# A gated attention and mixer kernel: w2's last 128 columns turned for three chunks, two weight loads later, the last output in three transfers

## The chip, the cores and the metric

The kernel runs on one core of one Trainium2 chip. The time is the device time of one execution in microseconds (us), and what is compared is the median of several runs.

## The reference, cut to what matters

The input x has 2048 tokens of 640 numbers (bfloat16). Two branches read it and a gate mixes them:

```python
g = sigmoid((x * gate_w).sum(-1))
a = linear_attention(x, wqkv) @ wo               # 32 heads of 20, phi(t) = t + 1 or exp(t)
h = gelu(layernorm(x) @ w1)
hs = shifted(h) @ w2                             # quarters of h's columns moved by +1, -1, +2, -2 tokens
x1 = x + hs
b = x1 + gelu(layernorm(x1) @ w3) @ w4           # w3 is 640 x 1728, w4 is 1728 x 640
out = g * a + (1 - g) * b
```

The change edits `x1 = x + hs`, the sums that the second layernorm takes from x1, and the moments at which w3 and w4 are loaded and the output's last tile is stored.

## The kernel before, in words

**Tiles.** Tokens are worked in 16 tiles of 128 and 4 chunks of 512; columns of 640 are 5 blocks of 128. Up to the second layernorm a chunk c has these steps, named as the planner's items are:

- `t1(u)`: a crossbar transpose (a DMA on SP's queue) of a normalized tile into `xnT`, so that columns lie on partitions.
- `w1(c, j)`, j = 0 to 4: five matmuls of 512 columns on TensorE (PE); ScalarE (ACT) takes the result through GELU into `hsT`, with the shift of tokens in the address. For j = 4 that is four pieces of 32 partitions.
- `w2(t)`: tile t's product with w2. For each of five blocks of `hsT` a matmul of 512 columns (L624), and one of the last 128 columns (L613) that keeps the same weights. VectorE (DVE) adds the 640 columns to `x_tok` and sums them for the layernorm (L662).
- `sq(t)`: ACT squares the tile and sums the squares (L680).
- `s2(c)`: GpSimd (POOL) makes mean and scale of four tiles from the sums, in eight small steps (`ln_chunk_stats`).
- `n2(u)`: POOL normalizes tile u into one of three buffers `xn`; `n2(u)` needs the buffer of `t2(u-3)` free.
- `t2(u)`: the crossbar transpose of that tile into `xnT`.
- `w3(c, j)`, j = 0 to 12: five matmuls of 512 columns (L605), GELU on ACT into `h2T`.

A chunk's last w2 tile needs the next chunk's last w1 group as well, for the shifted tokens. `w3(0, 3)` needs `w2(15)`.

**The attention branch meets this one** in the tiles `a(t)` (L1240), five matmuls each of `pqnT` with the small matrix `M_sb`. `pqnT` lies in the same memory as `hsT`. It is made by `qs(t)` and `qn(t)` on DVE (some 2.9 us a tile) and by the crossbar transpose `qt(t)`, which needs `w2(15)` and, for t < 6, `t2(11)`. Rows 60 to 67 of `M_sb` are copied from `Mt` by `mt`, five small DMAs on SP, planned after `qt(2)`. `qt(3)` and `t2(12)` are planned after `mt`. `w3(1, 7)` to `w3(1, 10)` are planned after `a(0)` to `a(3)`, one each; w4's products come after that.

**Order of work.** The program for each engine is written out by a planner at build time. It holds streams of items (W1, W2, SQ, S2, N2, T2, W3 and so on). Within a stream the order is fixed. Each item has a PE duration (1.08 for five matmuls of 512 columns, 1.33 for a w2 tile, 0 for an item without PE work) and dependencies with a lag (GEL = 1.3 behind a w1 group). The planner keeps a model of the engines' clocks. It issues the item that can start first by that model; among those, items without PE work go first, then the item with the longest remaining path of durations and lags:

```python
key = (max(est, t_pe), 0 if it["dur"] == 0.0 else 1, -cp[n])
```

On the chip every engine and every DMA queue then runs its list in order and waits on semaphores. So an instruction that waits holds up all that was planned behind it on its engine. SP's queue carries the crossbar transposes, the large loads of w3 and w4 and the output; the planner's model lets a crossbar land 2.8 us after its issue, whatever else is in flight.

**A turned product** exists already in the kernel for w4's last 128 columns (`w4_turned`): w4's block is the weights and 512 tokens are streamed. The result, with columns on partitions, goes through ACT into `mw` and by a crossbar transpose into `mtok`, four tiles at once, and DVE adds each tile's 128 columns.

**Loads.** w3 (one DMA, 2160 KB) and w4 (three DMAs, 2080 KB and twice 80 KB) are issued on SP, both before at about 89 us, behind `qb(3)` and `t1(15)`.

**The end.** The last tile's w4 product lies in two parts of PSUM, columns 0 to 384 and 384 to 512; the 128 turned columns are added first. Its output goes out in two transfers, columns 0 to 384 from ACT's queue and 384 to 640 from SP's.

Of the kernel before, what the change touches and what calls it, by code (L numbers as in the profile page):

```python
# [7 lines left out]
ACTF = mybir.ActivationFunctionType  # L8
ALU = mybir.AluOpType

S = 2048
D = 640
# [3 lines left out]
NT = S // 128  # L16
NCH = S // 512
KD = D // 128
# [398 lines left out]
def _build(nc, A_x, A_wqkv, A_wo, B_w1, B_w2, B_w3, B_w4, gate_w, out, dbg=None, stop=None):  # L417
    sch = _Sched(nc)
# [41 lines left out]
    ps = nc.alloc_psum_tensor("ps", [128, 8, 512], F32)  # L460
# [10 lines left out]
    st2 = pa.alloc("st2", [128, 8, NT], F32)  # L471
# [4 lines left out]
    w2 = pa.alloc("w2", [128, KD, D], BF16)  # L476
    wo_aug = pa.alloc("wo_aug", [128, 6, D], BF16)
    x_tok = pa.alloc("x_tok", [128, NT, D], BF16)
    xnT = pa.alloc("xnT", [128, KD, S], BF16)
    hsT = pa.alloc("hsT", [128, KD, S + 4], BF16)  # L480
# [28 lines left out]
    mw = rb.alloc("mw", [128, 2, 512], BF16)  # L509
    mtok = rb.alloc("mtok", [128, 2, 4, 128], BF16)  # L510
# [8 lines left out]
    def bank():  # L519
        best = None  # L520
        for k_ in range(nbanks[0]):
            b = (bank_rr[0] + k_) % nbanks[0]
            if b in bank_pend or b in bank_hold:
                continue
            lk = sch.locks.get(b)
            tfree = 0.0 if lk is None else sch.ev_time.get((lk[1].sem, lk[1].val), 1e18)
            if best is None or tfree < best[0]:
                best = (tfree, b)
        bank_rr[0] = best[1] + 1
        bank_pend.add(best[1])  # L530
        return best[1]
# [30 lines left out]
    def nfree(ap):  # L562
        n = 1
        for d_ in ap.shape[1:]:
            n *= d_
        return n

    def in_psum(ap):
        return ap.tensor.name == ps.name
# [8 lines left out]
    def dve(fn, reads, writes, cost=None):  # L578
        if cost is None:
            n = nfree(writes[0])  # L580
            cost = 65.0 + n / 0.96
        return sch.op("dve", fn, reads, writes, cost=cost)
# [7 lines left out]
    def pe(fn, reads, writes, cost=500.0, after=None):  # L590
        for w_ in writes:
            sp_, rl = sch.rects(w_)
            if sp_ == "ps":
                for (_p0, _p1, lo, hi) in rl:
                    for b in range(lo // PS_BANK, (hi - 1) // PS_BANK + 1):
                        bank_pend.discard(b)
        return sch.op("pe", fn, reads, writes, cost=cost, after=after)

    def mm_group(out_ap, pairs, reads_extra=()):
        n = len(pairs)  # L600

        def fn(e, out_ap=out_ap, pairs=pairs, n=n):
            ins = None
            for i, (l, r) in enumerate(pairs):
                ins = e.matmul(out_ap, l, r, start=(i == 0), stop=(i == n - 1))  # L605
            return ins
        reads = [a for p in pairs for a in p] + list(reads_extra)
        return pe(fn, reads, [out_ap], cost=n * (max(nfree(pairs[0][1]), 24) * 0.4167 + 2.5))
# [40 lines left out]
    def tt(engf, out_ap, a, b_, op):  # L649
        cost = None  # L650
        if engf is pool:
            cost = 1000.0 if op == ALU.pow else 200.0 + 2.3 * nfree(out_ap)
        elif not in_psum(a):
            cost = 830.0
        return engf(lambda e: e.tensor_tensor(out_ap, a, b_, op), [a, b_], [out_ap], cost=cost)  # L655

    def stt(out_ap, in0, scalar, in1, op0, op1, accum=None):
        rd = [in0, in1] + ([scalar] if not isinstance(scalar, (int, float)) else [])
        n = nfree(out_ap)
        cost = (65.0 + n / 0.96) if (in_psum(in0) or in_psum(in1)) else (160.0 + 1.04 * n)  # L660
        if accum is not None:
            return dve(lambda e: e.scalar_tensor_tensor(out_ap, in0, scalar, in1, op0, op1, accum_out=accum), rd,  # L662
                       [out_ap, accum], cost=cost + 70.0)
        return dve(lambda e: e.scalar_tensor_tensor(out_ap, in0, scalar, in1, op0, op1), rd, [out_ap], cost=cost)  # L664
# [3 lines left out]
    def activation(out_ap, in_ap, func, scale=1.0, bias=0.0, accum=None):  # L668
        rd = [in_ap] + [a for a in (scale, bias) if not isinstance(a, (int, float))]
        wr = [out_ap] + ([accum] if accum is not None else [])  # L670
        n = nfree(out_ap)
        cost = max(150.0, 100.0 + 0.833 * n + (70.0 if in_psum(in_ap) else 0.0)) + 45.0 * (len(rd) - 1)
        if accum is not None:
            cost += 91.0
        st_ = ACT_SET.get(func)
        if st_ is not None and st_ != sch.act_func:
            cost += 1290.0
            sch.act_func = st_
        if accum is not None:
            return act(lambda e: e.activation(out_ap, in_ap, func, bias=bias, scale=scale, accum_out=accum), rd, wr, cost=cost)  # L680
        return act(lambda e: e.activation(out_ap, in_ap, func, bias=bias, scale=scale), rd, wr, cost=cost)  # L681
# [106 lines left out]
    def tag_set(buf, sl, what):  # L788
        tags[(buf, sl)] = what

    def tag_chk(buf, sl, what):
        assert tags.get((buf, sl)) == what, ("stale ring slot", buf, sl, what, tags.get((buf, sl)))

    IT = _Items()
# [65 lines left out]
    def ln_chunk_stats(st, c, rs):  # L860
        cs = slice(4 * c, 4 * c + 4)
        ts(pool, st[:, 2, cs], rs, 1.0 / D, 0.0, ALU.mult, ALU.add)
        ts(pool, st[:, 3, cs], st[:, 1, cs], 1.0 / D, EPS_LN, ALU.mult, ALU.add)
        tt(pool, st[:, 4, cs], st[:, 2, cs], st[:, 2, cs], ALU.mult)
        tt(pool, st[:, 5, cs], st[:, 3, cs], st[:, 4, cs], ALU.subtract)
        tt(pool, st[:, 6, cs], st[:, 5, cs], negh[:, 0:4], ALU.pow)
        tt(pool, st[:, 7, cs], st[:, 2, cs], st[:, 6, cs], ALU.mult)
        ts(pool, st[:, 7, cs], st[:, 7, cs], -1.0, 0.0, ALU.mult, ALU.add)
# [101 lines left out]
    for i in range(3, NT + 2):  # L970
        if i < NT:
            addA(("q", i), 1.08, lambda t=i: q_tile(t))
            addA(("k", i), 1.36, lambda t=i: k_tile(t))
            if i % 4 == 3:
                addA(("qx", i // 4), 1.08, lambda c=i // 4: q_turned(c))
                IT.add("QB", ("qb", i // 4), 0.0, lambda c=i // 4: q_back(c),
                       deps=[(("qx", i // 4), 2.5), (("t1", NT - 1), 0.0) if i == NT - 1 else (("k", i + 1), 0.0)])
# [140 lines left out]
    def w2_tile(t):  # L1118
        tok = slice(2 + 128 * t, 2 + 128 * (t + 1))
        b = pair()  # L1120
        mm_both((ps[:, b, 0:512], ps[:, b + 1, 0:128]), [(hsT[:, k, tok], w2[:, k, 0:512], w2[:, k, 512:D]) for k in range(KD)])
        stt(x_tok[:, t, :], psf[:, 512 * b:512 * b + D], 1.0, x_tok[:, t, :], ALU.mult, ALU.add, accum=st2[:, 0, t:t + 1])

    def w2_sq(t):
        activation(junk[:, 0, :], x_tok[:, t, :], ACTF.Square, accum=st2[:, 1, t:t + 1])

# [206 lines left out]

    def out_tiles(t0, t1):
        dst = out[0, 128 * t0:128 * t1, :].rearrange("(n p) d -> p n d", p=128)
        for n0, n1 in ((0, 384), (384, D)) if t0 == NT - 1 else ((0, D),):
            sch.dma("act" if n1 == 384 else "sp", dst[:, :, n0:n1], x_tok[:, t0:t1, n0:n1], "out%d" % slot("out", 4))

    def w3_load():
# [9 lines left out]
    for c in range(NCH):  # L1349
        for j in range(KD):  # L1350
            deps = [(("t1", u), 0.9) for u in range(4 * c, 4 * c + 4)] if j == 0 else []
# [7 lines left out]
    for t in range(NT):  # L1359
        c = t // 4  # L1360
        deps = [(("w1", c, KD - 1), GEL)]
        if t % 4 == 3 and c + 1 < NCH:
            deps.append((("w1", c + 1, KD - 1), GEL))
        if t == 0:
            deps.append((("g", KD - 1), 0.0))
        IT.add("W2", ("w2", t), 1.33, lambda t=t: w2_tile(t), deps)
        IT.add("SQ", ("sq", t), 0.0, lambda t=t: w2_sq(t), [(("w2", t), 1.0)])
        if t % 4 == 3:
            IT.add("S2", ("s2", c), 0.0, lambda c=c: ln_chunk_stats(st2, c, st2[:, 0, 4 * c:4 * c + 4]), [(("sq", t), 1.0)])
    for u in range(NT):  # L1370
        deps = [(("s2", u // 4), 3.2 + 0.9 * (u % 4))]
        if u >= 3:
# [2 lines left out]
            deps.append((("t1", NT - 3 + u), 0.0))  # L1375
        IT.add("N2", ("n2", u), 0.0, lambda u=u: normalize(2, u, st2), deps)
        IT.add("T2", ("t2", u), 0.0, lambda u=u: t_xn(2, u), deps=[(("n2", u), 1.1)] + ([(("mt",), 0.0)] if u == 12 else []))
    IT.add("MISC", ("w3load",), 0.0, w3_load, deps=[(("qb", NCH - 1), 0.0), (("k", NT - 1), 0.0), (("t1", NT - 1), 0.0)])
    IT.add("MISC", ("w4load",), 0.0, w4_load, deps=[(("qb", NCH - 1), 0.0), (("kvt", 1), 0.0), (("t1", NT - 1), 0.0), (("z", NT - 1), 1.5)])
    for c in range(NCH):  # L1380
        for j in range(KFF):
            deps = []
# [4 lines left out]
            if j == 0:  # L1387
                deps = deps0 + [(("t2", u), 0.9) for u in range(4 * c, 4 * c + 4)]
# [12 lines left out]
    for t in range(NT):  # L1401
        deps = [(("zb",), 1.0), (("q", max(t, 2)), 2.0), (("sg", 1), 0.0)]
# [13 lines left out]
    for t in range(NT):  # L1416
        g = GOF[t]
        t0, t1 = GROUPS[g]
        cl = (t1 - 1) // 4
        deps = [(("qt", t), 3.0), (("w4load",), 0.0), (("m", 1), 1.0), (("mt",), 2.5)]  # L1420
# [66 lines left out]
```

## Time and profile before

| | us |
|---|---|
| median of 3 runs | 259.79 (259.15 to 259.86) |
| the profiled execution | 259.33 |
| its span, first to last instruction | 258.1 |
| PE busy | 255.2 |
| DVE busy | 143.3 |
| ACT busy | 108.5 |
| POOL busy | 90.1 |

PE's granted clock is full in every slice of the page. "PE" is the matmul stream and "PEld" the weight loads, which run beside it. A matmul of 512 columns is listed with 379 ns, but the matmuls are pipelined: the step from one start to the next is what it costs the stream. In a timeline each row has start, length, engine, line, operation, operands and count; `[idle ... <-...]` tells how long the engine stood still before it and what ended that. "SPq" is SP's queue; an issue's row has the time that issuing took, and the landing comes later. The median from issue to landing is 2.7 us for `xnT<-xn`, 2.4 us for `mtok<-mw`, 8.2 us for w3's load and 13.8 us for w4's largest.

### The profile page before, as it was taken

The page shows a single profiled execution, that of the slowest core. Times are in us where ns is not written, and L with a number is a line of the kernel's source. Part 1 is how long each engine was busy: PE and PEld are TensorE (multiplying, and loading weights), DVE is VectorE, ACT ScalarE, POOL GpSimd, SP SyncE. Part 2 cuts the span into 40 slices and gives each one's busy share as a digit, 9 for nine tenths or more (in the row PEclk, how much of TensorE's full clock was granted, in tenths as well). Part 3 has the DMA queues.
Part 4 walks back from the last instruction along what each step waited for, and adds up shares of the span by engine and source line. Part 5 has one row for each costly group of instructions (what it writes and reads, how often), then busy time and mean ns, then how long its engine had stood idle before and what let it go on. Part 6 is the DMA issues. An engine that isn't in the chain of part 4 may idle for free.

```text
span 258.1 us, 3609 instructions
## 1 busy us (share of the span) xinstructions
PE 255.2 (99%) x1418; PEld 111.0 (43%) x1242; DVE 143.3 (56%) x289; ACT 108.5 (42%) x222; POOL 90.1 (35%) x146
## 2 busy tenths in 40 slices
PE   8999999999999999999999999999999999999996
PEld 4333333344444333334444444444444444444444
DVE  2697888899953995489999400689300043200033
ACT  1496676751356867665854230003520100253000
POOL 5021399966772153667917100423000011300000
PEclk9999999999999999999999999999999999999999
DMA  6855599956843699562556631022300112200012
GB/s 206 245 136 105 180 182 131 268 116 127 109 97 79 97 338 358 106 101 56 108 55 125 122 61 20 0 79 76 51 0 0 23 20 102 102 1 3 0 20 102
DMA packets 57681, 26.48 MB, mean 103 GB/s; under 512 B 48916, under 2 KB 56253, under 8 KB 57664
## 3 DMA queue, kind: packets, MB, share of 16 engines
q1 hardware_dynamic: 54832, 21.87, 38.5%
q0 software_dynamic: 1168, 3.28, 5.8%
q10 hardware_dynamic: 1664, 1.11, 1.5%
q8 instruction: 10, 0.16, 0.3%
q14 instruction: 7, 0.06, 0.1%
HBM read 12.04 MB, written 2.62 MB: 57 GB/s over the span
## 4 chain that ended last, share of the span: by engine, by line
PE 99%; DVE 0%; issue 0%
PE ps L605 37%; PE ps L1240 30%; PE ps L624 14%; PE ps L831 7%; PE ps L613 4%; PE ps L942 2%; PE ps L904 1%; PE ps L1286 1%; PE ps L1147 1%; PE ps L636 1%; PE ps L1029 0%; PE ps L1058 0%; DVE x_tok L664 0%
## 5 line engine op out<-in xcount | busy, mean ns | idle before, releaser
L605 PE MATMUL ps<-xnT,w 128*128 128x512 bf16 x360 | 81.3, 379 | 0.0
L664 DVE SCALAR_TENSOR_TENSOR x_tok<-ps,stg,abx 128x512 bf16<-128x512 f32 (+2 forms) x17 | 12.2, 718 | 81.7 <-PE ps L1240 81.5
L681 ACT ACTIVATE h2T<-ps 128x512 bf16<-128x512 f32 x52 | 30.6, 598 | 59.3 <-PE ps L605 59.3
L605 PEld LDWEIGHTS ps<-xnT,w 128*128 128x128 bf16 x360 | 34.5, 98 | 41.6 <-issue 2.4
L1240 PE MATMUL ps<-w,h2T 128*128 128x512 bf16 (+2 forms) x221 | 45.4, 366 | 0.0
L647 POOL TENSOR_SCALAR xn<-x_tok,st 128x640 bf16<-128x640 bf16 x32 | 34.9, 1096 | 28.2 <-DMA xnT<-xn 27.6
L647 POOL TENSOR_SCALAR abx<-x_tok,stg 128x640 f32<-128x640 bf16 (+1 forms) x16 | 14.8, 933 | 70.2 <-DVE x_tok L664 70.2
L1240 PEld LDWEIGHTS ps<-w,h2T 128*128 128x128 bf16 x221 | 21.1, 98 | 24.1
L681 ACT ACTIVATE Er<-ps 128x512 bf16<-128x512 f32 (+1 forms) x36 | 23.0, 648 | 15.0 <-PE ps L613 10.7
L680 ACT ACTIVATE junk<-x_tok 128x640 bf16<-128x640 bf16 x32 | 23.6, 738 | 3.9 <-DVE x_tok L662 3.7
L681 ACT ACTIVATE hsT<-ps 128x512 bf16<-128x512 f32 (+1 forms) x32 | 19.0, 594 | 12.5 <-PE ps L605 12.0
L624 PE MATMUL ps<-w,hsT 128*128 128x512 bf16 x80 | 23.0, 379 | 0.0
L624 PE MATMUL ps<-wkg,xT 128*128 128x512 bf16 x70 | 20.7, 379 | 0.0
L662 DVE SCALAR_TENSOR_TENSOR x_tok<-ps,x_tok 128x640 bf16<-128x640 f32 x16 | 13.2, 822 | 11.0 <-PE ps L613 10.5
L1240 PE MATMUL ps<-M_sb,pqnT 128*128 128x512 bf16 (+2 forms) x85 | 18.6, 367 | 0.0
L831 PE MATMUL ps<-pk_tok,x_tok 128*128 128x512 bf16 x80 | 17.8, 379 | 0.0
L1176 DVE TENSOR_TENSOR pq_tok<-pq_tok,dnr 128x300 bf16<-128x300 bf16 (+1 forms) x48 | 17.4, 417 | 0.6
L613 PE MATMUL ps<-wkg,xT 128*128 128x130 bf16 x80 | 17.5, 219 | 0.0
L613 PE MATMUL ps<-w,hsT 128*128 128x128 bf16 x80 | 17.5, 219 | 0.0
L605 PE MATMUL ps<-wq,xT 128*128 128x512 bf16 x65 | 16.1, 379 | 0.0
L647 DVE TENSOR_SCALAR Er<-Er 128x512 bf16<-128x512 bf16 (+1 forms) x36 | 12.2, 339 | 7.0 <-ACT Er L681 6.3
L655 DVE TENSOR_TENSOR qprod<-qprod,pk_tok 128x640 f32<-128x640 f32 x13 | 15.2, 1166 | 0.4
(90 smaller groups left out, 252.6 us busy)
## 6 DMA issues: line engine op xcount, KB each, us to landing
w<-in_B_w_dram SPq DMA_DIRECT2D x1, 2160.0 KB, 8.2
w<-in_B_w_dram SPq DMA_DIRECT2D x1, 2080.0 KB, 13.8
out_dram<-x_tok SPq DMA_DIRECT2D x3, 640.0 KB, 3.2
w<-in_B_w_dram POOLq DMA_DIRECT2D x8, 160.0 KB, 6.2
x_tok<-in_A_x_dram SPq DMA_DIRECT2D x6, 160.0 KB, 3.9
x_tok<-in_A_x_dram SPq DMA_DIRECT2D x1, 960.0 KB, 5.4
wv<-in_A_wqkv_dram POOLq DMA_DIRECT2D x1, 800.0 KB, 5.6
x_tok<-in_A_x_dram SPq DMA_DIRECT2D x1, 640.0 KB, 4.6
```

Of the source, the lines that this page charges most:

```text
L605: ins = e.matmul(out_ap, l, r, start=(i == 0), stop=(i == n - 1))
L613: return e.add_instruction(mybir.InstMatmult(name=nc.get_next_instruction_name(), engine=e.engine, ins=[e.lower_ap(r), ll], outs=[e.lower_ ...
L624: e.matmul(outs[0], l, r, start=st, stop=sp, skip_group_check=True)
L647: return engf(lambda e: e.tensor_scalar(out_ap, in_ap, s1, s2, op0, op1), rd, [out_ap], cost=cost)
L655: return engf(lambda e: e.tensor_tensor(out_ap, a, b_, op), [a, b_], [out_ap], cost=cost)
L662: return dve(lambda e: e.scalar_tensor_tensor(out_ap, in0, scalar, in1, op0, op1, accum_out=accum), rd, [out_ap, accum], cost=cost + 70.0)
L664: return dve(lambda e: e.scalar_tensor_tensor(out_ap, in0, scalar, in1, op0, op1), rd, [out_ap], cost=cost)
L680: return act(lambda e: e.activation(out_ap, in_ap, func, bias=bias, scale=scale, accum_out=accum), rd, wr, cost=cost)
L681: return act(lambda e: e.activation(out_ap, in_ap, func, bias=bias, scale=scale), rd, wr, cost=cost)
L831: ins = e.matmul(o, l, r, start=(t0 + q_ == 0), stop=(t0 + q_ == NT - 1))
L1176: dve(lambda e, o=o, i0=i0, i1=i1: e.tensor_tensor(o, i0, i1, ALU.mult), [i0, dnr[:, 1, sd, :]], [o], cost=cost)
L1240: ins = e.matmul(o, l, r, start=first and i == 0, stop=last and i == len(prs) - 1, skip_group_check=True)
```

## The change

For chunks 0 to 2, a w2 tile multiplies only the first 512 columns (`w2_wide`); after a chunk's fourth tile one turned group (`w2_turned`, item `w2x(c)`) makes the last 128 columns for the chunk's 512 tokens. ACT copies it to `mw`, SP transposes it into `mtok`, and DVE adds it tile by tile (`w2_tail`, item `wt(u)`) with a sum of its own. The squares `sq(u)` of these tiles follow `wt(u)`, and `s2(c)` first adds the two sums on POOL. Chunk 3 stays as it was. w3's load is planned after `w2x(0)`, w4's after `w2x(2)` and `t2(7)`. The last tile's output goes out in three transfers: the turned columns 512 to 640 on SP, 0 to 384 on ACT, 384 to 512 on SP.

```diff
@@ -1121,6 +1121,33 @@
         mm_both((ps[:, b, 0:512], ps[:, b + 1, 0:128]), [(hsT[:, k, tok], w2[:, k, 0:512], w2[:, k, 512:D]) for k in range(KD)])
         stt(x_tok[:, t, :], psf[:, 512 * b:512 * b + D], 1.0, x_tok[:, t, :], ALU.mult, ALU.add, accum=st2[:, 0, t:t + 1])
 
+    W2T = 3
+
+    def w2_wide(t):
+        tok = slice(2 + 128 * t, 2 + 128 * (t + 1))
+        b = bank()
+        mm_group(ps[:, b, :], [(hsT[:, k, tok], w2[:, k, 0:512]) for k in range(KD)])
+        stt(x_tok[:, t, 0:512], ps[:, b, :], 1.0, x_tok[:, t, 0:512], ALU.mult, ALU.add, accum=st2[:, 0, t:t + 1])
+
+    def w2_turned(c):
+        sl = c % 2
+        b = bank()
+        mm_group(ps[:, b, :], [(w2[:, k, 512:D], hsT[:, k, 2 + 512 * c:2 + 512 * (c + 1)]) for k in range(KD)])
+        activation(mw[:, sl, :], ps[:, b, :], ACTF.Copy)
+        tag_set("mtok", sl, ("w2", c))
+        sch.dma("sp", mtok[:, sl, :, :], mw[:, sl, :], "trw%d" % sl, transpose=True)
+
+    def w2_tail(t):
+        c = t // 4
+        tag_chk("mtok", c % 2, ("w2", c))
+        stt(x_tok[:, t, 512:D], mtok[:, c % 2, t % 4, :], 1.0, x_tok[:, t, 512:D], ALU.mult, ALU.add, accum=st2[:, 3, t:t + 1])
+
+    def w2_sums(c):
+        cs = slice(4 * c, 4 * c + 4)
+        if c < W2T:
+            tt(pool, st2[:, 0, cs], st2[:, 0, cs], st2[:, 3, cs], ALU.add)
+        ln_chunk_stats(st2, c, st2[:, 0, cs])
+
     def w2_sq(t):
         activation(junk[:, 0, :], x_tok[:, t, :], ACTF.Square, accum=st2[:, 1, t:t + 1])
 
@@ -1333,7 +1360,7 @@
 
     def out_tiles(t0, t1):
         dst = out[0, 128 * t0:128 * t1, :].rearrange("(n p) d -> p n d", p=128)
-        for n0, n1 in ((0, 384), (384, D)) if t0 == NT - 1 else ((0, D),):
+        for n0, n1 in ((512, D), (0, 384), (384, 512)) if t0 == NT - 1 else ((0, D),):
             sch.dma("act" if n1 == 384 else "sp", dst[:, :, n0:n1], x_tok[:, t0:t1, n0:n1], "out%d" % slot("out", 4))
 
     def w3_load():
@@ -1363,10 +1390,17 @@
             deps.append((("w1", c + 1, KD - 1), GEL))
         if t == 0:
             deps.append((("g", KD - 1), 0.0))
-        IT.add("W2", ("w2", t), 1.33, lambda t=t: w2_tile(t), deps)
-        IT.add("SQ", ("sq", t), 0.0, lambda t=t: w2_sq(t), [(("w2", t), 1.0)])
+        turned = c < W2T
+        IT.add("W2", ("w2", t), 1.08 if turned else 1.33, lambda t=t: (w2_wide if t // 4 < W2T else w2_tile)(t), deps)
+        if turned and t % 4 == 3:
+            IT.add("W2", ("w2x", c), 1.08, lambda c=c: w2_turned(c), deps)
+            for u in range(4 * c, 4 * c + 4):
+                IT.add("WX", ("wt", u), 0.0, lambda u=u: w2_tail(u), [(("w2x", c), 3.6)])
+                IT.add("SQ", ("sq", u), 0.0, lambda u=u: w2_sq(u), [(("wt", u), 0.4)])
+        if not turned:
+            IT.add("SQ", ("sq", t), 0.0, lambda t=t: w2_sq(t), [(("w2", t), 1.0)])
         if t % 4 == 3:
-            IT.add("S2", ("s2", c), 0.0, lambda c=c: ln_chunk_stats(st2, c, st2[:, 0, 4 * c:4 * c + 4]), [(("sq", t), 1.0)])
+            IT.add("S2", ("s2", c), 0.0, lambda c=c: w2_sums(c), [(("sq", t), 1.0)])
     for u in range(NT):
         deps = [(("s2", u // 4), 3.2 + 0.9 * (u % 4))]
         if u >= 3:
@@ -1375,8 +1409,8 @@
             deps.append((("t1", NT - 3 + u), 0.0))
         IT.add("N2", ("n2", u), 0.0, lambda u=u: normalize(2, u, st2), deps)
         IT.add("T2", ("t2", u), 0.0, lambda u=u: t_xn(2, u), deps=[(("n2", u), 1.1)] + ([(("mt",), 0.0)] if u == 12 else []))
-    IT.add("MISC", ("w3load",), 0.0, w3_load, deps=[(("qb", NCH - 1), 0.0), (("k", NT - 1), 0.0), (("t1", NT - 1), 0.0)])
-    IT.add("MISC", ("w4load",), 0.0, w4_load, deps=[(("qb", NCH - 1), 0.0), (("kvt", 1), 0.0), (("t1", NT - 1), 0.0), (("z", NT - 1), 1.5)])
+    IT.add("MISC", ("w3load",), 0.0, w3_load, deps=[(("qb", NCH - 1), 0.0), (("k", NT - 1), 0.0), (("t1", NT - 1), 0.0), (("w2x", 0), 0.0)])
+    IT.add("MISC", ("w4load",), 0.0, w4_load, deps=[(("qb", NCH - 1), 0.0), (("kvt", 1), 0.0), (("t1", NT - 1), 0.0), (("z", NT - 1), 1.5), (("w2x", 2), 0.0), (("t2", 7), 0.0)])
     for c in range(NCH):
         for j in range(KFF):
             deps = []
```

## The prediction

> **What bounds the kernel now.** I read the page first: its head and the chain that ended last.
>
> ```profile
> span 258.1 us, 3609 instructions
> ...
> PE 99%; DVE 0%; issue 0%
> ```
>
> TensorE carries the end: 99% of the chain. Only matmul columns taken away, or a gap in the matmul stream, can move the time. Next the busy time by stretch, over the stage that the change edits (81 to 118 us) and the one behind it:
>
> ```profile
> 81.00:109.40 28.40, 28.40 (x178) 10.93 (x122) 20.73 (x50) 19.16 (x40) 10.54 (x20) 1.00 0.78 216
> 118.30:138.70 20.40, 20.40 (x109) 9.15 (x108) 19.39 (x45) 14.27 (x29) 11.22 (x16) 1.00 0.52 85
> ```
>
> The columns are the stretch, its length, busy PE, PEld, DVE, ACT, POOL, the clock and the DMA share with GB/s. PE is busy without a hole at clock 1.00, so there is no stall to win back. DVE is nearly full in the second stretch (19.39 of 20.40). Then PE's timeline where the last w1 group (L605 x5) gives way to w2 tiles 10 and 11:
>
> ```profile
> 106.92 1.24 PE L605 MATMUL ps<-xnT,w 128*128 128x512 bf16 x5
> 108.00 0.38 PE L624 MATMUL ps<-w,hsT 128*128 128x512 bf16 x1
> 108.22 0.22 PE L613 MATMUL ps<-w,hsT 128*128 128x128 bf16 x1
> 108.27 0.38 PE L624 MATMUL ps<-w,hsT 128*128 128x512 bf16 x1
> ...
> 109.36 2.32 PE L605 MATMUL ps<-xnT,w 128*128 128x512 bf16 x10
> 111.52 0.38 PE L624 MATMUL ps<-w,hsT 128*128 128x512 bf16 x1
> ```
>
> A 512-column matmul costs 0.216 us from start to start (108.00 to 108.22), the 128-column one behind it 0.055, a tile 1.36 (108.00 to 109.36). The two groups at 109.36 are already w3(0,0) and w3(0,1): they fill the time in which tile 11 waits for ScalarE's view of the last w1 group:
>
> ```profile
> 108.20 2.44 ACT L681 ACTIVATE hsT<-ps 32x512 bf16<-32x512 f32 x4 [1.12 <-PE ps L605]
> ```
>
> Last I looked for what becomes due after the stage. PE's first attention tile a(0) reads M_sb, whose rows 60 to 67 come by five small DMAs on SP's queue; behind that queue stands GpSimd's normalization:
>
> ```profile
> 114.86 0.54 POOL L647 TENSOR_SCALAR st<-st 128x4 f32<-128x4 f32 x1 [0.66 <-ACT junk L680]
> ...
> 118.27 2.61 POOL L647 TENSOR_SCALAR xn<-x_tok,st 128x640 bf16<-128x640 bf16 x3
> 121.83 1.80 POOL L647 TENSOR_SCALAR xn<-x_tok,st 128x640 bf16<-128x640 bf16 x1 [0.94 <-DMA xnT<-xn]
> ```
> ```profile
> 119.18 5.67 SPq L281 DMA_TRANSPOSE xnT<-xn  x4
> 124.89 3.92 SPq L281 DMA_TRANSPOSE pqnT<-pq_tok  x3
> 128.91 4.07 SPq L285 DMA_DIRECT2D M_sb<-Mt  x5
> ```
> ```profile
> 138.51 1.24 PE L1240 MATMUL ps<-M_sb,pqnT 128*128 128x512 bf16 x5
> ```
>
> SP runs in order and back to back here: t2(8..11), qt(0..2), M_sb. t2(11) is the fourth transpose; it starts at 123.65 (the 1.20 us before 124.89, and a 0.04 gap). M_sb's last issue ends at 132.98; with 1.6 us of landing (the 64 KB output's row) M_sb is there at 134.6. PE asks at 138.5. **So the slack of t2(11) is 3.9 us**, and w3(1,7) is held behind a(0) in the items' dependencies: PE has nothing else then.
>
> **The change, part by part.** *PE's columns.* Per chunk, 20 matmuls of 128 columns (20 x 0.056 = 1.12 us) go and 5 of 512 come (5 x 0.216 = 1.08): the same columns. Gain 0.04 a chunk, 0.13 us in all. (The Trainium skill, "TensorE: Matmul & The Clock Gate", section "Back-to-back issue gap", gives about 81 ns for a 128-column matmul in a stream with its weight loads; by that the gain would be 60 x 0.081 - 3.24 = 1.6 us. The row says 0.055, as the second matmul here keeps the weights, so the rule is not used.)
>
> *Order on PE.* The planner issues by longest remaining path, with its own costs; I use these for order alone. The turned path adds 1.08 + 3.6 + 0.4 to a chunk, yet w1 and w2 still merge one by one. Through tile 10, eleven tiles lose 0.28 each and two turned groups add 1.08 each: tile 10 ends at 109.36 - 0.95 = 108.4. The last w1 group now ends two wide tiles earlier, 106.25, and its hsT is ready 2.65 later (108.00 to 110.64 before): 108.95. w3(0,0) can't fill the hole, since chunk 0's t2(3) comes later than 108.5 (next part). **A gap of 0 to 0.55 us; I take 0.55.** Tile 11 ends at 110.0, the turned group of chunk 2 at 111.1, tiles 12 to 15 at 116.6.
>
> *Chunk 0's and 1's longer path* (copy, crossbar, tail add, square) delays t2(0..3) from 108.5 to about 113 to 117 and t2(4..7) from 117 to about 123. PE has tiles 12 to 15 until 116.6 and w3's chunk 0 (13 x 1.08) until 131. The crossbar of chunk 2 stands ahead of t2(3) on SP and waits for ACT's copy; PE may wait up to 0.5 us there, which the next part swallows. Nothing else is charged.
>
> *Chunk 2's path, where the money is.* Before: tile 11 ended at 112.88, t2(11) started at 123.65. Now from 111.1:
> - Copy on ACT: 0.2 + 0.6 gives 111.9 at once; behind chunk 1's four squares, ready just before (four of 0.92, 0.73 + 0.19, from 108.95), 113.2. I take 113.2.
> - Crossbar 0.1 + 2.4 (row of mtok): 114.4 to 115.7.
> - Four tail adds on DVE, 0.34 + 0.08 each, 1.7: 116.1 if they go at once; behind the adds of tiles 12 to 15, the last ending at 116.6 + 0.2 + 0.8 = 117.6, 119.3. I take 119.3: when the planner's crossbar lands, tile 15 is already issued.
> - Squares: the last 0.92 behind its add, 117.0; or four in a row from 118.1 with two GELUs of w3 (0.5 each) between them, 122.7. I take 122.7.
> - GpSimd's sums: 114.86 to 118.27 was 3.4, and one 0.2 is added: 120.6 to 126.3.
> - n2(8) 0.9, t2(8) 2.6 to land, n2(11), which reuses that buffer, 0.9 (the row at 118.27, a third of 2.61) to 1.8 (the row at 121.83), 0.1: t2(11) at 125.1 to 131.7. I take 0.9 as the commoner, so 130.8.
> - The queue behind it as before, 123.65 to 134.6 = 10.9: M_sb at 136.0 to 142.6, by my choices **141.7**. PE asks at 138.5 - 0.1 + 0.55 = 138.9.
>
> So PE idles between nothing and 3.7 us at a(0), and I take 2.8: three of the four choices (squares ahead, adds ahead, ACT full) follow from in-order queues that were full in the profile.
>
> *The loads.* w3's (one DMA) is issued behind the first crossbar, about 94 instead of 89.5, and lands 8.2 later, 14 us before its first use. w4's (three DMAs) goes behind t2(7), about 122, needed at 151.7; even 13.8 us is enough. But they share SP's queue:
>
> ```profile
> w<-in_B_w_dram SPq DMA_DIRECT2D x1, 2080.0 KB, 13.8
> ```
> ```profile
> DMA to landing us min/median/max: 4.2/6.6/7.6
> ```
>
> The second line is the transposes issued at 97 to 103, in the shadow of the two loads; those at 119 to 124 took 2.6 (all four). The shadow moves from t2(0..2) to t2(8..10). Alone, w4's 2.1 MB at some 300 GB/s (2160 KB and 2080 KB landed by 104 after 89.5) takes 7 us, to 129: t2(8), issued at 127, lands 0 to 2 us later than counted. I take 0; 2 goes into the range.
>
> *Output.* The last transfer shrinks from 64 to 32 KB. By the rows (64 KB 1.6, 96 KB 1.7, 160 KB 1.8) that gives 0.05 us; one more issue on SP (0.4) lies earlier. Bounds -0.1 and +0.1. (The Trainium skill, "DMA: Bandwidth & Descriptors", "Specifications", puts the line rate at 512 bytes or more, with a read-modify-write below; the rows of 128 columns now are 256 bytes, so by it the sum would gain nothing here. No row of before has such an output.)
>
> **Sum**, on the profiled execution's own 259.33 us (span 258.1 and 1.2 around it): -0.13 + 0.55 + 2.8 - 0.05 = +3.2, 262.5. The median of the runs, 259.79, lies 0.46 above that execution; shifted by that the forecast is **263.0 us**.
>
> **Rivals.** *Not slower: the slack holds.* If the tail adds get ahead of tiles 12 to 15 on DVE and the squares run as they land, t2(11) starts by 127.9 (123.65 + 3.9 + the 0.4 that PE is later) and a(0) finds M_sb. For it: the low ends above give 125.1, and tile 11 itself runs 2.9 us earlier. Against: all three queues must be free at once. Then the time is 259.79 - 0.18 to + 0.37: 259.6 to 260.2. Chance 0.24. *The load in the way.* At 90.67 in SP's timeline an issue of w4 lasted 5.5 us behind w3's load. If SP stands like that behind w4's load, or t2(8) lands 5 late (7.6 against 2.6), t2(11) moves to 133 or more and a(0) to 144: 265 to 266. Against: w3's bytes are gone by then. Chance 0.13. *The change does nothing on PE*: a turned group has the columns of what it replaces, which is the 0.13 already in the sum; it can't be over 0.2, so faster by 0.3% (0.78 us, about what a measurement of this kernel can tell from no change) needs a gain that no row shows: 0.03. The forecast case, 1 to 4 us of waiting, has 0.60.
>
> Range: 259.6 to 265.0. It takes in the holding case, leaves out the gain and most of the load case, some 2 in 10. The forecast case's own range is 261 to 264.5. Same takes 0.23, slower 0.74.
>
> **What would show it.** Right: PE's first hole at about 108.4, up to 0.6 us, released by ACT hsT; a hole of 2 to 4 us before the first M_sb<-pqnT matmul, released by DMA M_sb; M_sb's five issues at 136 to 141 instead of 129 to 133; t2(8..11) at 127 to 131; 60 hsT matmuls fewer on L613, 15 more of 512 columns on L605. From there to the end the stream must keep its length (119.6 us from 138.5). Wrong: PE at 99 to 100% through 139 us, or the hole elsewhere, for instance at w3(0,0) near 116.6 for w3's load, or t2(11) before 128 although the squares ran late.

## The result and the profile after

The changed kernel takes 267.38 us (median of 6 runs, 265.97 to 268.46), the kernel before 259.7 us beside it: a ratio of 1.0301, 95% interval 1.0273 to 1.0329. The forecast was 263.0 us with a range up to 265.0: slower, as forecast, but by 7.7 us and not by 3.2. The profiled execution of the changed kernel is the slowest of the six, 268.46 us; its own excess over the profiled execution of before (259.33) is 9.1 us.

The page of the kernel after, its head, two of its 40-slice rows and the chain that ended last:

```profile
span 267.2 us, 3601 instructions
...
PE   8899999999999999999893999999999999999997
...
PEclk9999999999999999999997799999999999999999
...
PE 90%; ACT 5%; issue 2%; DMA 2%; SPq 0%; DVE 0%; ACTq 0%
```

A slice is 6.7 us. The PE row has a notch, 8 9 3, in the slices from 127 to 147 us; the clock row has 7 7 in the two from 140 to 154 us, where before it had nines throughout. PE carries 90% of the chain instead of 99%. The waits of PE, with total, number and longest in us:

```profile
PE ps L1267 <- issue: 4.6, 1, 4.6
PE ps L1058 <- ACT h2T L681: 1.0, 1, 1.0
...
PE ps L605 <- ACT hsT L681: 0.4, 1, 0.4
```

L1267 is the line that was L1240 before. PE's timeline shows where they lie:

```profile
106.46 2.32 PE L605 MATMUL ps<-w,hsT 128*128 128x512 bf16 x10
109.15 1.04 PE L605 MATMUL ps<-w,hsT 128*128 128x512 bf16 x4 [0.36 <-ACT hsT L681]
...
128.70 0.74 PE L1058 MATMUL ps<-wo_aug,Lt 60*64 60x512 bf16 x16 [0.99 <-ACT h2T L681]
129.37 10.96 PE L605 MATMUL ps<-xnT,w 128*128 128x512 bf16 x50
144.91 2.29 PE L1267 MATMUL ps<-M_sb,pqnT 128*128 128x512 bf16 x5 [4.58 <-issue]
147.00 2.34 PE L605 MATMUL ps<-xnT,w 128*128 128x512 bf16 x5
```

Three holes. Measured as steps from start to start beyond what the matmul costs, they are 0.53 us behind 108.40, 1.16 behind 127.33 and 4.74 behind 139.96. The last ends with a(0), the first M_sb<-pqnT matmul, at 144.91 instead of 138.51. And the five matmuls of a(0) take 2.29 us where before five took 1.24. The windows around a(0) say why (columns as in the prediction: stretch, length, busy PE, PEld, DVE, ACT and POOL, clock, DMA share and GB/s):

```profile
140.20:144.90 4.70, 0.13 (x1) 0.02 (x1) 4.46 (x11) 0.60 (x1) 0.74 (x1) 0.89 0.06 13
144.90:148.10 3.20, 3.19 (x8) 1.14 (x9) 3.06 (x8) 0.00 (x0) 0.00 (x0) 0.50 0.70 139
148.10:151.20 3.10, 3.10 (x9) 1.07 (x8) 0.76 (x3) 0.60 (x1) 0.87 (x2) 0.58 0.60 120
151.20:160.00 8.80, 8.80 (x49) 3.98 (x49) 0.00 (x0) 3.04 (x6) 0.77 (x1) 1.00 0.63 125
```

PE stood for 4.7 us, and then the granted clock is half for some six microseconds: 8 matmuls in 3.20 us, where at full clock 15 would go. The loss is (1 - 0.50) x 3.20 + (1 - 0.58) x 3.10 = 2.9 us, with PE listed as fully busy.

So the 9.1 us of the profiled execution are in two parts. a(0) is 6.4 us later: 0.2 because the work before the edited stage lies that much later in this execution (50.80 instead of 50.63 for the same matmul), +0.5, +1.2 and +4.7 for the holes, and -0.13 for the columns. From a(0) to the end it takes 122.3 us (267.2 - 144.91) instead of 119.6: +2.7, the clock.

SP's queue shows what a(0) waited for:

```profile
113.36 1.19 SPq L281 DMA_TRANSPOSE mtok<-mw  x1
116.48 5.43 SPq L281 DMA_TRANSPOSE xnT<-xn  x4
121.96 2.19 SPq L285 DMA_DIRECT2D w<-in_B_w_dram  x3
126.96 8.39 SPq L281 DMA_TRANSPOSE xnT<-xn  x4
135.39 3.92 SPq L281 DMA_TRANSPOSE pqnT<-pq_tok  x3
139.41 4.21 SPq L285 DMA_DIRECT2D M_sb<-Mt  x5
```

t2(8..11) took 8.39 us of the queue instead of 5.67, M_sb's five issues end at 143.62 instead of 132.98. The trace names no releaser for a(0) (`issue`). That it is M_sb shows in the order of times: here and in nine of the kernels below, all those with a hole at a(0), it starts 1.2 to 1.3 us after the end of M_sb's fifth issue, and in qt_early and msb_first the row names DMA M_sb. Two views more belong to this lateness. The landing of the three transposes issued from 127.0 to 129.5, t2(8..10):

```profile
DMA to landing us min/median/max: 3.9/4.7/5.2
```

and POOL's timeline over the same time:

```profile
125.64 3.02 POOL L647 TENSOR_SCALAR xn<-x_tok,st 128x640 bf16<-128x640 bf16 x3
128.63 0.47 POOL L647 TENSOR_SCALAR st<-st 128x4 f32<-128x4 f32 x2
...
131.25 0.19 POOL L647 TENSOR_SCALAR st<-st 128x4 f32<-128x4 f32 x1
132.28 2.28 POOL L647 TENSOR_SCALAR xn<-x_tok,st 128x640 bf16<-128x640 bf16 x2 [0.84 <-DMA xnT<-xn]
```

n2(8..10) run at 125.64, then chunk 3's sums (`s2(3)`, the `st<-st` steps) until 131.44, and n2(11) starts at 132.28, released by the landing of t2(8). It has two things ahead of it that end within a microsecond of each other. In the kernel before, these sums came behind n2(11), the prediction's row at 121.83:

```profile
123.59 0.48 POOL L647 TENSOR_SCALAR st<-st 128x4 f32<-128x4 f32 x2
```

In the changed kernel the planner's order has them ahead of it.

### The profile page after: what moved, and what is told of

It is laid out like the page before. It is cut to its first block, busy times and chain, and to the rows that moved or that the text cites. A ratio compares the mean times of both kernels' runs of the same rounds, so it can differ in the third digit from the quotient of the medians.

```text
span 267.2 us, 3601 instructions
## 1 busy us (share of the span) xinstructions
PE 257.7 (96%) x1373; PEld 112.3 (42%) x1257; DVE 144.5 (54%) x313; ACT 110.8 (41%) x225; POOL 90.5 (34%) x149
## 4 chain that ended last, share of the span: by engine, by line
PE 90%; ACT 5%; issue 2%; DMA 2%; SPq 0%; DVE 0%; ACTq 0%
PE ps L605 39%; PE ps L1267 30%; PE ps L624 8%; PE ps L831 6%; ACT junk L680 2%; PE ps L613 2%; DMA x_tok<-in_A_x_dram 2%; PE ps L942 1%; ACT h2T L681 1%; PE ps L1313 1%; ACT hsT L681 1%; PE ps L1174 1%; SPq L285 0%; PE ps L1058 0%; PE ps L1029 0%
## 5 line engine op out<-in xcount | busy, mean ns | idle before, releaser
L605 PE MATMUL ps<-xnT,w 128*128 128x512 bf16 x360 | 82.7, 383 | 0.0
L1267 PE MATMUL ps<-w,h2T 128*128 128x512 bf16 (+2 forms) x221 | 45.4, 367 | 0.0
L1267 PEld LDWEIGHTS ps<-w,h2T 128*128 128x128 bf16 x221 | 21.1, 98 | 24.1
L1267 PE MATMUL ps<-M_sb,pqnT 128*128 128x512 bf16 (+2 forms) x85 | 20.4, 392 | 4.6 <-issue 4.6
L681 ACT ACTIVATE mw<-ps 128x512 bf16<-128x512 f32 x7 | 4.2, 597 | 29.5 <-PE ps L1267 28.9
L662 DVE SCALAR_TENSOR_TENSOR x_tok<-ps,x_tok 128x512 bf16<-128x512 f32 (+1 forms) x16 | 11.4, 718 | 9.2 <-PE ps L605 8.4
L605 PE MATMUL ps<-w,hsT 128*128 128x512 bf16 x60 | 14.8, 379 | 0.4 <-ACT hsT L681 0.4
```

The costliest lines, as they stand in the source:

```text
L1267: ins = e.matmul(o, l, r, start=first and i == 0, stop=last and i == len(prs) - 1, skip_group_check=True)
```

## The experiments

**The theory** from the two traces: a(0) is late because t2(11) is late, and t2(11) is late for three reasons in a row: chunk 2's squares and sums, as forecast; w4's load, behind which t2(8) is issued; and chunk 3's sums on POOL. The half clock behind the hole is a cost of its own. **Rivals:** the load explains the excess alone; the low clock is not the hole's doing; the loads or the output, not the turned product, carry part of it. Each kernel is the changed one with the edit shown, if nothing else is said.

**w4_with_w3**: w4's load goes out right behind w3's, at the first crossbar.

```diff
-    (("z", NT - 1), 1.5), (("w2x", 2), 0.0), (("t2", 7), 0.0)])
+    (("z", NT - 1), 1.5), (("w2x", 0), 0.0)])
```

> The changed kernel with one difference: w4's three DMAs are issued right behind w3's (near 95 us) instead of behind t2(7) (122 us). Theory (chunk 2's transposes wait behind w4's load, and that lateness reaches M_sb): t2(8) lands 2.6 us after its issue near 127 instead of 5.2, SP issues t2(11) without being held, M_sb's issues end near 140.3 instead of 143.6, the first M_sb matmul starts near 141.7 instead of 144.9, the hole before it is 1 to 2 us, the clock stays at 1.00, and the time is 261.5 to 263. Rival (the turned path alone makes the lateness, the load's place costs nothing): M_sb's issues end past 142.5, time 266 or more.

Measured: 266.91 us, ratio 1.0282 (1.0248 to 1.0315), not to be told from the changed kernel. The expected 261.5 to 263 was missed; the time and the end of M_sb's issues lie where the rival had put them. Landing of the three transposes issued at 127.6 to 130.2, then POOL, then SP:

```profile
DMA to landing us min/median/max: 2.6/2.7/2.7
```
```profile
129.26 0.48 POOL L647 TENSOR_SCALAR st<-st 128x4 f32<-128x4 f32 x2
...
132.47 3.14 POOL L647 TENSOR_SCALAR xn<-x_tok,st 128x640 bf16<-128x640 bf16 x3
```
```profile
127.59 6.99 SPq L281 DMA_TRANSPOSE xnT<-xn  x4
134.62 4.64 SPq L281 DMA_TRANSPOSE pqnT<-pq_tok  x3
139.36 4.14 SPq L285 DMA_DIRECT2D M_sb<-Mt  x5
```

The shadow is gone, 2.6 us to landing instead of 3.9 to 5.2, and yet M_sb's issues end at 143.5, as before the edit: n2(11) now stands behind chunk 3's sums until 132.47, though its buffer was free from 130.15. One cover was taken away and the next held the same instruction. So the rival is not the whole account either: the load does make t2(8) late, but another wait, one that ended 0.8 us sooner, stands beside it. The load itself now shadows t2(0..2), n2(3) and t2(3) wait behind them, and w3(0,0) waits 1.39 us at 113.6 for DMA xnT, a hole that the changed kernel hasn't.

**sums3_late** and **w4_and_sums3**: chunk 3's sums are planned behind n2(11), alone and with the edit above.

```diff
-    lambda c=c: w2_sums(c), [(("sq", t), 1.0)])
+    lambda c=c: w2_sums(c), [(("sq", t), 1.0)] + ([(("n2", 11), 0.0)] if c == 3 else []))
```

> The changed kernel with one order changed on GpSimd: chunk 3's eight small sums are planned behind n2(11) instead of ahead of it. Theory (two waits stand side by side in front of n2(11): these sums, done at 131.4, and t2(8)'s landing behind w4's load, 132.2): alone it gives nothing, M_sb's issues still end near 143.6, time 266 to 268.5. Rival (the sums are the wait that counts): M_sb's issues end by 142, time 265.5 or less.

> Both at once: w4's load right behind w3's, and chunk 3's sums behind n2(11). Theory (each wait hides the other, so only both together move M_sb): n2(11) starts at 130.3, t2(11) is issued at 131.2, M_sb's issues end near 141.3, the hole before the first M_sb matmul is 1 to 2 us, clock 1.00, time 262.8 to 264.2. Rival (a third wait stands beside them): M_sb's issues end past 142.5, time 265.5 or more.

Measured: alone 266.96 us, 1.0290 (1.0253 to 1.0328), nothing, M_sb's issues ending at 143.87. Together 263.75 us (single runs 263.01 to 265.66), 1.0174 (1.0131 to 1.0218). POOL and SP of w4_and_sums3:

```profile
129.45 0.87 POOL L647 TENSOR_SCALAR xn<-x_tok,st 128x640 bf16<-128x640 bf16 x1 [0.95 <-DMA xnT<-xn]
```
```profile
126.80 5.16 SPq L281 DMA_TRANSPOSE xnT<-xn  x4
132.00 4.77 SPq L281 DMA_TRANSPOSE pqnT<-pq_tok  x3
136.87 4.14 SPq L285 DMA_DIRECT2D M_sb<-Mt  x5
```

n2(11) starts 2.8 us earlier than in the changed kernel, M_sb's issues end at 141.01, the hole before a(0) is 1.98 us and the clock stays at 1.000 in every run. Alone neither edit moves the time by more than half a microsecond, and both together give back 3.6 us (3.3 by the ratios to the kernel before): the two waits stood side by side on n2(11). Between the two profiled executions (268.46, the slowest of its kernel, and 263.01, the fastest of its own) a(0) comes 2.6 us earlier (142.29), and the stream from there to the end is 2.8 us shorter (119.5), which is the clock; how the 3.6 of the medians splits is not measured. What is left is four holes: 0.53 as before, 0.99 at 113.25, where w3(0,0) waits for t2(3) in the load's shadow, 1.04 for ACT's h2T and 1.98 for M_sb. In this kernel M_sb's last issue ends within a microsecond of where the prediction's chain put it (141.7 less 1.6 of landing, 140.1).

**fill_wait**: 20 matmuls on constants stand in PE's list ahead of a(0); they compute nothing that is used.

```diff
     def a_tile(t):
+        if t == 0:
+            warmup(512 * 20, 0.42)
```

> The changed kernel with 20 extra matmuls of 512 columns on constants (4.3 us, into an unused PSUM bank) in front of the first M_sb matmul, where PE stands still for 4.7 us. Theory (the stop itself halves PE's clock for the 15 to 30 matmuls behind it): the M_sb matmul starts at the same 144.9, the steps behind it are 0.216 and not 0.427 us, the granted clock stays 1.00, and the time falls by 1.5 to 2.8 us to 264.7 to 266. Rival (the slow steps come from what the matmuls read or write there, not from the stop): the steps stay at 0.427 and the time is 267.4 or more.

Measured: 265.34 us, ratio 1.0240 (1.0216 to 1.0264), clear of the changed kernel's interval, clock 1.000 in every run. PE, and the windows:

```profile
139.78 4.54 PE L904 MATMUL ps<-const-bfloat16-1.0 128*128 128x512 bf16 x20
144.16 1.24 PE L1269 MATMUL ps<-M_sb,pqnT 128*128 128x512 bf16 x5
```
```profile
139.80:144.10 4.30, 4.30 (x21) 1.97 (x20) 4.09 (x11) 0.60 (x1) 0.00 (x0) 1.00 0.08 17
144.10:151.20 7.10, 7.10 (x35) 3.21 (x33) 3.46 (x9) 1.56 (x3) 1.75 (x3) 1.00 0.66 131
```

The wait is nearly as long as it was (139.78 to 144.16), only filled, and the stream behind it keeps 0.216 us a matmul. That settles the clock: it is the standing still of PE that costs it, not the work of this stage. From a(0) to the end it is 119.5 us here and 122.3 in the changed kernel: 2.8 us between the two profiled executions. Of the median it is up to 2.0 us (267.38 - 265.34; 1.6 by the ratios). Up to, because a(0) itself comes 0.75 us earlier in the profiled execution, where M_sb's issues end at 142.74.

**qt_early**: qt(0..2) need t2(7) instead of t2(11).

```diff
-    (("t2", 11 if t < 6 else NT - 1), 0.0)]
+    (("t2", 7 if t < 3 else 11 if t < 6 else NT - 1), 0.0)]
```

> The changed kernel with the planner's dependency of qt(0..2) moved from t2(11) to t2(7), so qt(0..2) and M_sb's five DMAs need not stand behind chunk 2's transposes. Theory (M_sb behind the late t2(8..11) is what PE waits for, and nothing else of chunk 2 is due before 150 us): no hole at the first M_sb matmul, clock 1.00; what remains is the 0.5 us at 108.4 and about 1 us where m_first waits for ACT: time 260.3 to 261.5. Rival (the late chunk stops PE at the next place as well, a later w3 group or half group): a hole of over 1 us behind 140 us, time 263 or more.

Measured: 267.05 us, 1.0284 (1.0250 to 1.0318), a miss. SP:

```profile
128.59 10.59 SPq L281 DMA_TRANSPOSE xnT<-xn  x4
139.28 4.11 SPq L285 DMA_DIRECT2D M_sb<-Mt  x5
```

qt(0..2) did go out at 122.3, but the planner then put w4's load and t2(8..11) in their place ahead of `mt`, and M_sb's issues begin at 139.28, as before the edit. t2(8), now straight behind the load, landed 7.6 us after its issue. An order-only edit moved the wait, because the thing that was late still stood ahead of M_sb.

**msb_first**: qt(0..2) as in qt_early but behind w4's load in the order, and `mt` planned ahead of t2(11) instead of t2(12).

```diff
-    [(("mt",), 0.0)] if u == 12 else []
+    [(("mt",), 0.0)] if u == 11 else []
-    (("t2", 11 if t < 6 else NT - 1), 0.0)]
+    (("t2", 7 if t < 3 else 11 if t < 6 else NT - 1), 0.0)] + ([(("w4load",), None)] if t < 3 else [])
```

> The changed kernel, all three chunks turned, with two dependencies of the planner moved: qt(0..2) behind t2(7), and t2(11) behind M_sb's five DMAs, so that these no longer stand behind chunk 2's last transpose on SP. Theory (PE's long hole is only this queue order): M_sb's issues end by 136, no hole over 0.5 us at the first M_sb matmul, clock 1.00; the 0.5 us at 108.4 and about 1 us at m_first remain: time 260.5 to 261.8. Rival (the late chunk 2 costs the same at its next use): a hole over 2 us later, time 264 or more.

Measured: 261.95 us, 1.0099 (1.0076 to 1.0122), clock 1.000. SP and PE:

```profile
124.31 7.04 SPq L281 DMA_TRANSPOSE pqnT<-pq_tok  x3
131.44 4.75 SPq L281 DMA_TRANSPOSE xnT<-xn  x3
136.32 4.14 SPq L285 DMA_DIRECT2D M_sb<-Mt  x5
```
```profile
141.72 1.25 PE L1267 MATMUL ps<-M_sb,pqnT 128*128 128x512 bf16 x5 [0.75 <-DMA M_sb<-Mt]
```

With t2(11) no longer ahead of M_sb, the last hole shrinks from 4.74 to 0.91 us and two thirds of the loss are gone. It is a near miss (expected 260.5 to 261.8): M_sb's issues end at 140.46 and not by 136, because right behind w4's load qt(0..2) take 7.04 us of the queue instead of 3.92. Three holes of 0.53, 0.69 (w3(0,0), for t2(3)) and 1.09 us (for ACT's h2T) remain; with the last one and the columns, 0.53 + 0.69 + 1.09 + 0.91 - 0.13 = 3.1, and the profiled execution is 262.45, 3.1 above that of before.

**Parts of the change alone.** out_only is the kernel before with only the three output transfers; loads_only the kernel before with only the loads moved (w3's behind w2(3), w4's behind w2(11) and t2(7)).

```diff
-    ((0, 384), (384, D)) if t0 == NT - 1
+    ((512, D), (0, 384), (384, 512)) if t0 == NT - 1
```

> The kernel before with only the last tile's output in three transfers. Theory: the last landing comes 0.1 us earlier (1.46 instead of 1.56 from issue), one more issue on SP lies before it; time 0.05 us lower, between -0.1 and +0.1, not to be told from no change. Rival (rows of 256 bytes are slower): +0.2 us or more.

```diff
-    (("t1", NT - 1), 0.0)])                         # w3load
+    (("t1", NT - 1), 0.0), (("w2", 3), 0.0)])
-    (("z", NT - 1), 1.5)])                          # w4load
+    (("z", NT - 1), 1.5), (("w2", 11), 0.0), (("t2", 7), 0.0)])
```

> The kernel before with only the loads moved: w3's behind tile 3, w4's behind t2(7) and tile 11; nothing turned. Theory: t2(8..11) lie behind w4's load and land up to 3 us later, but t2(11) had 3.9 us to spare: no hole over 0.5 us, time 259.2 to 260.3. Rival (the load's place is the cause by itself): a hole of 2 us or more before the first M_sb matmul, time 262 or more.

Measured: out_only 0.9997 (0.9985 to 1.0009), loads_only 0.9998 (0.9975 to 1.0021). Neither has a cost alone that these intervals show (some 0.3 and 0.6 us wide to each side). loads_only has the same shadow (t2(8..10) landing 3.3 to 4.7 us after issue), but M_sb's issues end at 135.2, well ahead of PE: the load is only a cost where the turned product has eaten the slack. The rivals that give the excess to the loads or the output alone fall.

**Fewer turned chunks.** turned_2 turns chunk 2 alone (w3's load then waits for w2(3), as there is no first crossbar), turned_01 chunks 0 and 1 (w4's load behind w2(11) and t2(7)), turned_01_w4 the same with w4's load at the first crossbar, turned_0 chunk 0 alone with that load.

```diff
-    W2T = 3                      # chunks with c < W2T are turned
+    W2T = 2                      # turned_01 and turned_01_w4; 1 in turned_0
-        if c < W2T:
+        if c == 2:               # turned_2, at all three places
```

> The changed kernel with only chunk 2 turned; chunks 0 and 1 as before, the loads late. Theory (chunk 2's path alone carries the loss): M_sb's issues end at 141 or later, a hole of 2.5 to 5 us before the first M_sb matmul, half clock behind it in most runs, time 264 to 267.5. Rival (the squares of chunk 1, bunched on ACT by its turning, are needed for the lateness): the hole is under 2 us, time 262 or less.

> The changed kernel with only chunks 0 and 1 turned; chunk 2 is made as before, and w4's load stays late (behind t2(7) and tile 11). Theory (chunk 2's longer path is what makes M_sb late): t2(11) is issued by 128, no hole before the first M_sb matmul, clock 1.00, time 259.3 to 260.5. Rival (the late load of w4, which stays, is what makes M_sb late): a hole of 2 us or more before the first M_sb matmul, time 262 or more.

> Chunks 0 and 1 turned as in the run of that kind, but w4's load right behind w3's. There t2(9) to t2(11) were issued behind w4's load and landed 6 to 8 us later, and M_sb's issues ended at 145.9. Theory (in that kernel the load's place is the cause): the transposes land in 2.6, M_sb's issues end by 141, the hole before the first M_sb matmul is under 1.5 us; the holes of 1.3 and 1.7 us near 109 and 115 stay: time 261.5 to 264. Rival (the order that the planner chose for chunks 1 and 2 is the cause, not the load): M_sb's issues end past 143, time 266 or more.

> Only chunk 0 turned, both large loads right behind the first crossbar, the output in three transfers. Theory (the columns are the same, so a turned chunk gains 0.04 us, and chunk 0's lateness meets tiles 12 to 15 and no wait): time 259.2 to 260.4, not to be told from before, with at most a hole of 0.5 us near 108. Rival (any turned chunk makes M_sb late): a hole of 2 us or more before the first M_sb matmul, time 262 or more.

Measured: turned_2 264.9 us, 1.0210 (1.0188 to 1.0232); turned_01 270.41, 1.0427 (1.0407 to 1.0447); turned_01_w4 266.13, 1.0241 (1.0202 to 1.0280); turned_0 261.45, 1.0066 (1.0040 to 1.0093). a(0) in turned_2:

```profile
142.24 1.24 PE L1267 MATMUL ps<-M_sb,pqnT 128*128 128x512 bf16 x5 [2.78 <-issue]
```

Chunk 2 alone gives the first hole (0.53) and one of 2.94 before a(0): the forecast's two holes. So 5.3 of the 7.7 us are there with chunk 2 turned alone, as expected; its longer path and w4's load, late here too, are not told apart by it. That leaving chunk 2 as it was would save the rest was wrong: turned_01, expected at 259.3 to 260.5, is the slowest of all. SP in turned_01:

```profile
127.28 2.20 SPq L285 DMA_DIRECT2D w<-in_B_w_dram  x3
130.14 6.79 SPq L281 DMA_TRANSPOSE xnT<-xn  x3
...
141.72 4.16 SPq L285 DMA_DIRECT2D M_sb<-Mt  x5
```

The planner put w4's load behind t2(8), straight ahead of t2(9..11), which landed 6.2 to 8.3 us after their issue; PE stands for 5.82 us before a(0), and two more holes open (1.33 and 1.71 us, for ACT's hsT and h2T). With the load out of the way (turned_01_w4) 4.3 us come back, and the two holes stay. But that run missed its expectation (261.5 to 264) and has the rival's numbers: M_sb's issues end at 143.95, and PE stands for 3.08 us before a(0). POOL's timeline there shows why: n2(8) at 125.47, then chunk 3's sums from 126.60, and n2(9) only at 130.03. It is the second wait of the changed kernel again, now ahead of n2(9) and not of n2(11). And one turned chunk (turned_0) still costs 1.6 us, where none was expected. PE in turned_0:

```profile
110.68 0.39 PE L624 MATMUL ps<-w,hsT 128*128 128x512 bf16 x1 [1.16 <-ACT hsT L681]
...
140.61 1.24 PE L1267 MATMUL ps<-M_sb,pqnT 128*128 128x512 bf16 x5 [0.61 <-issue]
```

Its tiles of chunk 1 to 3 are those of before, but by the trace PE reaches the tile that needs the last w1 group before ACT's view of it is there, and nothing else is ready. No turned version reaches the kernel before (turned_0 is the nearest), and by the columns none could beat it by much: the change has 0.13 us of them to win.

## Why the prediction was right or wrong

**Right: the columns, the first hole, the output, the place of the loss.** The hole behind 108.4 us, released by ACT hsT, was put at 0.55 and measured 0.53 in every kernel with chunk 2 turned. The output's three transfers were put at -0.05; out_only cannot tell them from nothing. The loss was put at a(0), which waits for M_sb, at the end of a chain through the crossbar, the tail adds, the squares, POOL's sums and SP. Down to t2(8) that chain holds to a quarter of a microsecond where it was counted out: copy until 113.3 (113.2), last tail add 119.2 (119.3), t2(8) issued 126.96 (127.2). A part of the last is luck: n2(8) started 0.7 earlier than the chain has it (125.64 and not 126.3) and took 1.3 us instead of 0.9. (For the first hole the text subtracts 0.95 where its own terms give 0.92, and adds 2.65 to 106.25 as 108.95; put right, 0.55 becomes 0.48.) The choices "behind the adds of tiles 12 to 15" and "four in a row" were right: the queues were full.

**Wrong: "t2(8), issued at 127, lands 0 to 2 us later than counted. I take 0; 2 goes into the range."** It landed at 132.19, 5.2 us after issue, and not 2.6. t2(11) started at 133.2 and not at 130.8, and its issue took 2.2 us instead of 1.2; with the queue behind it, M_sb came some 3.5 us later (its issues end at 143.62, the forecast's at about 140). Why t2(11)'s issue was slow, when w4's load had landed by 131.9, is open. The row of 4.2 to 7.6 us "in the shadow of the two loads" was the right price and stood in the text; it was set aside because the loads' bytes were counted at 300 GB/s, w4 gone by 129. It landed from 131.3 on, 9.3 us after its issue, some 225 GB/s. The rival "the load in the way", t2(8) 5 late, was nearer than the forecast, at 265 to 266, but it is not the account either: with the load moved away M_sb's issues still ended at 143.50 (w4_with_w3).

**Not seen: chunk 3's sums on POOL.** The step "n2(11), which reuses that buffer, 0.9" (to 1.8) took POOL as free when t2(8) lands, as it was in the kernel before. Chunk 3's squares finish at that time too, and its sums, 2.8 us, stand ahead of n2(11). In the changed kernel they lay beside the wait for t2(8), which is why they cost nothing there, and why taking the load away alone gained nothing. Both together, with the clock that hangs on them, are 3.6 us of the median, shown by w4_and_sums3. This and the load are the two steps of the chain that failed.

**Not priced: the clock behind the hole.** "From there to the end the stream must keep its length (119.6 us from 138.5)": it took 122.3. The prediction saw the clock at 1.00 and a hole of 2.8 us ahead of a(0) and never put the two together. That is up to 2.0 us of the median and 2.8 between the profiled executions (fill_wait). In turned_01_w4 a hole of 3.08 us was enough to lower the clock, so the forecast's own hole of 2.8 was close enough for a term in the range. The Trainium skill has a rule on it ("TensorE: Matmul & The Clock Gate", section "Part 1: The HAM clock gate (the "warmup" mystery)"): half clock after an idle window of some 3.4 us, and the window runs free. The runs agree with the half clock and with its length (below), but not with 3.4 us as the least hole that costs it.

**Not seen, and probably free here: the hole behind 127.3.** 1.16 us for ACT's h2T. Ahead of it ACT runs eight squares, chunk 2's and chunk 3's, between 118.4 and 125.7, with one GELU among them. In the changed kernel it moves the work ahead of a(0) later, and since a(0) waits for M_sb, that wait should be shorter by as much. In turned_2, where the eight squares end 0.8 us earlier and have two GELUs among them, it is not there. That the squares are its cause is read from the trace; no run moved them alone.

The sum by what was measured, for the profiled execution: -0.13 + 0.53 + 1.16 + 4.74 + 2.7 + 0.2 = 9.2, against 9.1. The forecast had -0.13 + 0.55 + 2.8 - 0.05 = 3.2: its wait at a(0) was 1.9 too small, and the hole for h2T and the clock stood in it at nothing.

## What to carry to other kernels

A turned product with the same matmul columns saves nothing on TensorE and adds a copy, a crossbar and an add to the path of every tile: count the slack of the last consumer, here 3.9 us, before the columns. When a wait is removed and the time stays, look at what stands beside it: two waits of equal length each hide the other, and only both together show their price. And price a hole in a full matmul stream twice, once for itself and once for the clock behind it; where a hole can't be removed, matmuls on constants in it keep the clock.

## What the runs showed of the hardware

**The clock falls in portions.** Where PE stood, the mean clock of a run is one of three values, 1.000, 0.994 or 0.987. The first columns are the profiled execution's, the last lists all runs:

| kernel | hole before a(0), us | mean clock | a(0) to the end, us | clock of all runs |
|---|---|---|---|---|
| w4_and_sums3 | 1.98 | 1.000 | 119.5 | 1.000 in 4 |
| turned_2 | 2.94 | 1.000 | 119.5 | 1.000 in 1, 0.994 in 3, 0.987 in 1 |
| turned_01_w4 | 3.08 | 0.994 | 120.8 | 1.000 in 2, 0.994 in 2 |
| w4_with_w3 | 3.57 | 0.994 | 121.2 | 1.000 in 1, 0.994 in 3 |
| qt_early | 3.61 | 0.994 | 121.1 | 1.000 in 1, 0.994 in 2, 0.987 in 1 |
| sums3_late | 4.67 | 0.987 | 122.4 | 0.994 in 3, 0.987 in 1 |
| changed kernel | 4.74 | 0.987 | 122.3 | 0.994 in 3, 0.987 in 3 |
| turned_01 | 5.82 | 0.987 | 121.8 | 0.987 in 4 |

By the windows around a(0), 0.987 is 6.8 us at half clock: 2 x (0.11 x 4.70 + 0.50 x 3.20 + 0.42 x 3.10). 0.994 is half of that. One portion cost the stream behind a(0) 1.3 to 1.7 us, two cost 2.3 to 2.9. Single runs go the same way (turned_2: 262.96, then 264.54 to 265.14, then 266.43), but not only the clock moves them: w4_and_sums3 has 263.01 to 265.66 with 1.000 in all. A hole of 2 us never cost a portion here, one of about 3 us none, one or two, one of 4.7 one or two, one of 5.8 always two. The half clock can start after a(0) (w4_with_w3: a(0) at 144.78, clock 1.00 until 145.5 and 0.50 from 145.6) or while PE still stands, as in turned_01_w4:

```profile
142.20:144.60 2.40, 0.14 (x1) 0.00 (x0) 2.30 (x7) 0.60 (x1) 0.00 (x0) 1.00 0.05 13
144.60:145.20 0.60, 0.00 (x0) 0.00 (x0) 0.56 (x2) 0.00 (x0) 0.00 (x0) 0.51 0.08 15
145.20:148.00 2.80, 2.75 (x7) 1.02 (x8) 2.66 (x8) 0.00 (x0) 0.00 (x0) 0.50 0.63 126
```

Only one run of each kernel has a trace, so the holes of the others are not known. If they are the same, a number that changes from run to run fits a window that runs free of the kernel; no run tests that. One run of the kernel before (262.15 us) shows 0.993 without any such change, and has no trace.

**A crossbar transpose issued behind a large load on the same queue lands only after it.** 2.6 us from issue to landing alone, 3.9 to 5.2 behind w4's load (issued 5.0 us earlier, landed at 131.3, t2(8) at 132.2), 6.2 to 8.3 directly behind it in turned_01 (load at 136.8, transposes from 137.9 on). Issuing slows as well, from 1.2 or 1.3 us to as much as 2.7 (turned_01). Whether it is the queue or the load's traffic was not separated: all these loads and transposes went out on SP.

**Rows of 256 bytes show no cost at this size.** The 32 KB output with such rows landed in 1.5 us, the 64 KB one of before in 1.6, and the time did not move (out_only, to some 0.3 us). The Trainium skill's limit of 512 bytes for the line rate ("DMA: Bandwidth & Descriptors", "Specifications") does not show here; a transfer this small says little about the rate, and no run had the same bytes in both row lengths.

Left open: how the time would split between the 0.53 hole, the one for ACT's h2T and a(0) if each were removed by itself, and why the planner's order differs as it does between turned_01 and the changed kernel, which was only read from the traces.
